# One sampling pass of four wide lag segments and one lag table, in place of two passes and two tables

## The chip, the cores and the metric

The kernel runs on one core of a Trainium2 chip. The metric is the device time in microseconds (us) of one execution. Engines are named as in the profile: PE (matrix products), DVE (elementwise work with two inputs, statistics), ACT (one-input functions, copies out of PSUM), POOL (GpSimd), SP (here only DMA issues). "PEclk" is the share of PE's full clock that was granted.

## The reference, cut to what matters

```python
# x: 1 x 2048 x 512, bf16; N = 128 states per channel
h  = x + A(layernorm(x))      # a state-space convolution over 2048 positions, per channel
h2 = h + B(layernorm(h))      # h @ w1 -> gelu -> @ w2, along the positions (2048 -> 1792 -> 2048)

# inside A, for each of 512 channels d:
P = exp(dt * A * l)                                # l = 0..2047
K = einsum("dn,dnl,dn->dl", C, P, dt * B).real     # the convolution kernel
y = causal_convolution(u, K) + u * Dskip           # by FFT in the reference
```

The kernel computes no FFT over 2048. It cuts the positions into 16 chunks of 128. Inside a chunk and its neighbour it works with exact spectra. Everything farther away goes through a **far field**: K is smooth enough in the lag to be interpolated from samples. The samples are taken on **segments** of the lag axis: around a segment's centre, K is a sum over the states of (a coefficient `cmu`) x (a table `T` of exponentials at 11 nodes). A product with a coefficient `mu` moves the centre one segment on.

Of the kernel before, what the change touches and what calls it, by code (L numbers as in the profile page):

```python
# [17 lines left out]
HR = 158.0  # L18
NR = 7
NQ = 11  # L20
NH = 5
QS = 12
NJ = 8
SEL0 = 100
SELW = 228
CA = 6
RA = 3
NA = (0, 6)
ROW = [QS * r if r < RA else 64 + QS * (r - RA) for r in range(NR)]
TQ = 88  # L30
# [18 lines left out]
def _tables():  # L49
    xh = np.cos(np.pi * np.arange(NH) / (NQ - 1))  # L50
    xh[2] = P / HR
    xq = np.concatenate([xh, -xh, [0.0]])
    tau = 63.5 + 64 * np.cos(np.pi * (2 * np.arange(NJ) + 1) / (2 * NJ))
    s = np.arange(P)
    om = np.pi * (2 * np.arange(64) + 1) / P
    co, si = np.cos(np.outer(s, om)), np.sin(np.outer(s, om))
    lb = _lagrange(tau, s)

    def wts(l):
        R = np.clip(np.floor(l / (2 * HR)), 0, NR - 1).astype(int)  # L60
        w = np.zeros((P,) + l.shape)
        for r in range(NR):
            w[ROW[r]:ROW[r] + NQ] = np.where(R == r, _lagrange(xq, (l - HR * (2 * r + 1)) / HR), 0)
        return w

    near = wts(s.astype(float))[:NQ]
    phi = [near @ co, near @ si]
    t = {}
    t["dft"] = np.concatenate([co, si], 1)
    t["lwin"] = np.zeros((P, 56))  # L70
    t["lwin"][:, 24:32] = lb.T
    selphi = np.zeros((P, 8, 2, P))
    selw = np.zeros((P, 8, SELW))
    for j in range(8):
        for q in range(NQ):
            for cs in range(2):
                selphi[8 * q + j, j, cs, 0:64] = phi[cs][q]
                selphi[8 * q + j, j, cs, 64:128] = phi[cs][q]
            selw[8 * q + j, j, SEL0 + q] = 1.0
    t["selphi"] = selphi.reshape(P, -1)  # L80
    t["selw"] = selw.reshape(P, -1)
    r = 15 - np.arange(16)
    wi = np.zeros((P, NJ, P))
    for i in range(NJ):
        lag = (128.0 * r[:, None] + tau[i] - tau[None, :]).reshape(-1)
        later = np.repeat(r > 0, NJ) * 1.0
        wi[:, i] = wts(lag + 128) + wts(np.maximum(lag, 0)) * later
    t["wi"] = wi.reshape(P, -1)
    t["inv1"] = np.concatenate([co.T, si.T], 0) / 64
    t["inv2"] = np.concatenate([si.T, -co.T], 0) / 64  # L90
    lrep = np.zeros((P, 4, P))
    for f in range(4):
        lrep[32 * f:32 * f + 32, f] = np.tile(lb, (4, 1))
    t["lrep"] = lrep.reshape(P, -1)
    off, cols = {}, []
    o = 0
    for k, v in t.items():
        off[k] = (o, v.shape[1])
        o += v.shape[1]
        cols.append(v)  # L100
    tab = np.concatenate(cols, 1).astype(ml_dtypes.bfloat16)
    msk = np.zeros((P, 4), np.float32)
    for p in range(P):
        msk[p, (p // 8) % 4] = 1.0
    return tab, off, msk, xh
# [54 lines left out]
class Op:  # L160
    __slots__ = ("i", "eng", "emit", "cost", "deps", "dma", "rd", "wr", "tag", "pos", "sig", "waits",
                 "mode", "name", "prio", "sec", "cols", "cw", "ins")


ENGINES = ("pe", "act", "dve", "pool", "sp")
LAT = 190.0
SAME = {"pe": 0.0, "act": 95.0, "dve": 125.0, "pool": 100.0, "sp": 0.0}
TICK = 10240 / 3
DMA_LAT = 1900.0
ISSUE = 480.0  # L170
MODE_NS = 70.0
TABLE_NS = 1280.0
RUN = 1024
RATE = {"raw": 275, "X": 275, "Mb": 275, "W2": 350}
WARM = (8000.0, 48000.0)


class Rec:



    def __init__(self, nc):
        self.nc = nc
        self.ops = []
        self.pages = {}
        self.bankops = {}
# [7 lines left out]
    def add(self, eng, emit, reads, writes, cost, dma=False, after=(), tag="", mode=None, name="", cols=0, share=1.0):  # L194
        o = Op()
        o.i = len(self.ops)
        o.eng, o.emit, o.cost, o.dma, o.tag, o.mode, o.name = eng, emit, cost, dma, tag, mode, name
        o.sec, o.cols, o.cw = self.sec + ":" + eng, cols, cols * share
        o.prio = PRIO.get(o.sec, self.base)
        if not name and writes and hasattr(writes[0], "tensor"):  # L200
            o.name = writes[0].tensor.name
        on_chip = lambda a: hasattr(a, "tensor") and not isinstance(a.tensor, bass.DRamTensorHandle)
        o.rd = [footprint(a) for a in reads if on_chip(a)]
        o.wr = [footprint(a) for a in writes if on_chip(a)]
        deps = set(x.i for x in after if x is not None)
        for is_w, fs in ((0, o.rd), (1, o.wr)):
            for f in fs:
                for b in banks(f):
                    for (q, qw) in self.bankops.get(b, ()):
                        if q in deps:  # L210
                            continue
                        if self.ops[q].eng != eng or eng == "pe" or is_w or qw:
                            deps.add(q)
                if f[0]:
                    continue
                for pg in self.pageset(f):
                    for (q, qw, qf) in self.pages.get(pg, ()):
                        if (is_w or qw) and q not in deps and overlap(f, qf):
                            deps.add(q)
        for is_w, fs in ((0, o.rd), (1, o.wr)):  # L220
            for f in fs:
                for b in banks(f):
                    self.bankops.setdefault(b, []).append((o.i, is_w))
                if not f[0]:
                    for pg in self.pageset(f):
                        self.pages.setdefault(pg, []).append((o.i, is_w, f))
        deps.discard(o.i)
        o.deps = sorted(deps)
        self.ops.append(o)
        return o  # L230
# [44 lines left out]
    def schedule(self):  # L275
        ops = self.nodes()
        n = len(ops)
        succ = [[] for _ in range(n)]
        for o in ops:
            for d in o.deps:  # L280
                succ[d].append(o.i)
        order = {e: [] for e in ENGINES}
        fin = [0.0] * n
        start = [0.0] * n
        nd = [len(o.deps) for o in ops]
        ready_t = [0.0] * n
        avail = {e: 700.0 for e in ENGINES}
        mode = {e: "exp" if e == "act" else None for e in ENGINES}
        dma_free = 0.0
        ticks = {}  # L290
        pend = {e: [] for e in ENGINES}
        for o in ops:
            if nd[o.i] == 0:
                pend[o.eng].append(o.i)
        left = n
        while left:
            best = None
            for e in ENGINES:
                if not pend[e]:
                    continue  # L300
                t0 = min(max(avail[e], ready_t[i]) for i in pend[e])
                if best is None or t0 < best[0]:
                    best = (t0, e)
            t0, e = best
            cand = [i for i in pend[e] if max(avail[e], ready_t[i]) <= t0]
            i = min(cand, key=lambda i: (ops[i].prio + (0 if ops[i].mode in (None, mode[e]) else 2), i))
            soon = [j for j in pend[e] if ops[j].prio < ops[i].prio - 0.3
                    and ready_t[j] < t0 + 0.5 * ops[i].cost and j not in cand]
            if soon and e != "pe" and not ops[i].dma:
                i = min(soon, key=lambda j: (ready_t[j], j))  # L310
            o = ops[i]
            pend[e].remove(i)
            t0 = max(t0, ready_t[i])
            if o.mode is not None and o.mode != mode[e]:
                t0 += MODE_NS if e == "pe" else TABLE_NS
                mode[e] = o.mode
            start[i] = t0
            cost = o.cost
            if e == "pe":
                tk = int(t0 // TICK)  # L320
                cost = o.cost if WARM[0] <= t0 < WARM[1] or ticks.get(tk - 1, 0) >= 3060 else o.cols
                ticks[tk] = ticks.get(tk, 0) + o.cw
            if o.dma:
                avail[e] = t0 + ISSUE
                dma_free = max(dma_free, t0) + o.cost
                fin[i] = dma_free + DMA_LAT
            else:
                avail[e] = t0 + cost
                fin[i] = t0 + cost
            order[e].append(i)  # L330
            left -= 1
            for s in succ[i]:
                nd[s] -= 1
                lat = SAME[e] if ops[s].eng == e and not o.dma else LAT
                ready_t[s] = max(ready_t[s], fin[i] + lat)
                if nd[s] == 0:
                    pend[ops[s].eng].append(s)
# [1035 lines left out]
```

## The kernel before: what the change and the argument touch

The segments are 316 lags wide (twice HR = 158), so 7 of them (NR) cover the axis. Coefficients `cmu` for segment r come from those of earlier segments by complex products with powers of mu, four of them single and one triple:

```python
# params(), on DVE; cuts marked ...
tt(m[:, :, :], SCm, bc2(Em), M)                 # mu^128
ts(self.p1[:, :], m[:, 0], 1.0, A)              # 1 + its real part
tt(self.num[:, :, :], self.cb[:, :, :], bc2(self.p1[:, :]), M)
tt(self.nb[:, :, :], self.cb[:, :, :], bc2(m[:, 1]), M)
tt(self.num[:, 0], self.num[:, 0], self.nb[:, 1], A)
tt(self.num[:, 1], self.num[:, 1], self.nb[:, 0], S)
...
for lv in range(3):                             # mu^2, mu^4, mu^8 by squaring
    ...
cprod(cm[:, :, 0:1], self.num[:, :, :].unsqueeze(2), 0, 1)
...
cprod(cm[:, :, 1:2], cm[:, :, 0:1], 1, 1)
cprod(cm[:, :, 2:3], cm[:, :, 1:2], 1, 1)
cprod(cm[:, :, 3:4], cm[:, :, 1:2], 2, 1)
cprod(cm[:, :, 4:7], cm[:, :, 0:3], 3, 3)
```

PE turns tables and coefficients into samples `g`, picks out the right ones with 0/1 matrices ("selections", `kt`), and interpolates a lag table `G` from them. G times the shifted moments `Mb` of the input gives the far field `O`. All this is done twice: segments 0 to 2 for the first 6 chunks, segments 3 to 6 for the other 10.

```python
def samples(self, hf):                          # hf = 0: three segments, hf = 1: four
    for nb in range(4):
        for gl in range(16):
            for c in range(2):
                mm(..., self.T[:, c, nb // 2, o:o + P], cm[:, c, 16 * nb + gl], ...)  # 128 products
        b.act(self.g[...], ...)                 # ACT copies them out of PSUM
    ...                                         # selections, copied into kt
def far(self, hf):
    for i in range(0, NJ, 2):                   # four pairs of nodes
        for q in range(2):
            b.mm(self.bank(bb + q), self.tb("wi", (i + q) * P, P), self.kt[:, :])
        b.act(dst, src, AF.Copy)                # G, 1024 columns, all four on ACT
    for s in range(32):
        for q in range(4):                      # the lag product, 128 small matmuls
            b.mm(..., Gv[:, q, s], Mv[:, q, s])
    ...                                         # O = result times a mask: 8 and 12 evictions, 12 of them on DVE
```

Behind it each chunk's output y takes the near product, the spectrum product and the far-field product on PE; DVE adds it to X; a second norm yields `H`; and H times the weights W1 and W2 fills PE to the end. The kernel orders its own instructions by a table of priorities.

## Time and profile before

The median of the three runs before the prediction was 164.92 us (164.78 to 165.16). The profiled execution is another one, with a span of 162.1 us.

| engine | busy us | what fills it |
|---|---|---|
| PE | 152.3 (94%) | real products, and 22.1 us of filler that reads only `idf`, all before 50 us |
| DVE | 139.7 | tables and coefficients in front, then y, norms and combinations of W1 |
| ACT | 84.6 | sines and exponentials, then PSUM evictions |
| POOL | 0.7 | nothing but constants |

There are 4062 instructions. I take the filler for no bound, since it stands where PE would otherwise wait.

### The profile page before, as it was taken

What the parts mean: (1) busy time and instruction counts of PE and PEld (TensorE: products, weight loads), DVE (VectorE), ACT (ScalarE), POOL (GpSimd) and SP (SyncE); (2) the same over time, 40 slices, a digit from 0 to 9 for tenths busy, and PEclk for the clock granted to TensorE, in tenths of its full rate; (3) what the DMA queues carried; (4) which work ended last, traced back from release to release, by engine and by line L of the source; (5) the groups of instructions that cost most, each with busy time, mean ns of one, the idle gap of its engine ahead of it and who ended that gap; (6) DMA issues with size and microseconds to landing.
All of it is one profiled execution on the core that took longest, in us unless ns stands there. A gap on an engine that the chain in (4) does not pass through costs nothing.

```text
span 162.1 us, 4062 instructions
## 1 busy us (share of the span) xinstructions
PE 152.3 (94%) x1705; PEld 112.9 (70%) x1705; DVE 139.7 (86%) x334; ACT 84.6 (52%) x201; POOL 0.7 (0%) x6
## 2 busy tenths in 40 slices
PE   7689958799989999999999999999999999999994
PEld 4569843468376753855544678888888888888883
DVE  3698999999999799999999999999999975384853
ACT  1799999898979899417467443158330000000000
POOL 1000000000000000000000000000000000000000
PEclk9999999999987999999999999999999999999999
DMA  4999999921407200069999000000000112102023
GB/s 122 349 383 401 400 405 398 405 91 53 145 20 239 93 0 0 4 210 418 406 411 363 14 0 0 0 4 0 0 0 4 34 42 89 34 32 69 32 69 126
DMA packets 12160, 23.78 MB, mean 147 GB/s; under 512 B 989, under 2 KB 8158, under 8 KB 12014
## 3 DMA queue, kind: packets, MB, share of 16 engines
q1 hardware_dynamic: 10558, 22.02, 36.6%
q10 hardware_dynamic: 1584, 1.51, 2.9%
q8 instruction: 13, 0.21, 0.5%
q14 instruction: 5, 0.04, 0.1%
HBM read 21.29 MB, written 2.35 MB: 146 GB/s over the span
## 4 chain that ended last, share of the span: by engine, by line
PE 68%; ACT 18%; DVE 10%; ACTq 1%; issue 1%
PE ps L485 68%; ACT SC L492 3%; DVE T L508 3%; ACT G L492 3%; DVE cmu L508 3%; ACT E L492 2%; ACT L498 2%; ACT H L492 2%; ACTq L542 1%; ACT junk L492 1%; DVE ct L508 1%; ACT g L492 1%; DVE X L522 1%; ACT kt L492 1%; ACT UF L492 1%
## 5 line engine op out<-in xcount | busy, mean ns | idle before, releaser
L485 PE MATMUL ps<-H,W 128*128 128x512 bf16 (+1 forms) x184 | 33.2, 328 | 0.0
L485 PEld LDWEIGHTS ps<-H,W 128*128 128x128 bf16 x184 | 17.4, 98 | 11.5 <-DVE H L518 0.9
L768 PE MATMUL ps<-idf 128*128 128x256 bf16 x154 | 22.1, 298 | 1.1 <-POOL idf L533 1.1
L485 PE MATMUL ps<-gT,W 128*128 128x256 bf16 x182 | 23.0, 273 | 0.0
L768 PEld LDWEIGHTS ps<-idf 128*128 128x128 bf16 x154 | 16.0, 107 | 4.9 <-POOL idf L533 1.1
L485 PEld LDWEIGHTS ps<-gT,W 128*128 128x128 bf16 x182 | 17.6, 98 | 2.2
L508 DVE TENSOR_TENSOR X<-ps,acc 128x256 bf16<-128x256 f32 x24 | 9.8, 421 | 7.2 <-PE ps L485 7.1
L508 DVE TENSOR_TENSOR W<-W 128x1024 bf16<-128x1024 bf16 (+1 forms) x23 | 14.7, 656 | 0.5 <-PE ps L485 0.4
L485 PE MATMUL ps<-HT,W 128*128 128x256 bf16 x112 | 14.2, 273 | 0.0
L522 DVE SCALAR_TENSOR_TENSOR acc<-ps,b2T,X 128x256 f32<-128x256 f32 x24 | 11.3, 478 | 3.1 <-PE ps L485 2.9
L492 ACT ACTIVATE H<-X 128x512 bf16<-128x512 bf16 x16 | 9.9, 619 | 5.5 <-DVE X L522 5.5
L522 DVE SCALAR_TENSOR_TENSOR X<-ps,X 128x512 bf16<-128x512 f32 x16 | 10.7, 687 | 1.4 <-PE ps L485 1.2
L485 PEld LDWEIGHTS ps<-HT,W 128*128 128x128 bf16 x112 | 10.9, 98 | 1.3
L485 PE MATMUL ps<-TS,S 128*128 128x256 bf16 x84 | 11.3, 273 | 0.0
L485 PE MATMUL ps<-TS,W 128*128 128x256 bf16 x84 | 11.0, 273 | 0.0
L492 ACT ACTIVATE UF<-ps,ub 128x512 bf16<-128x512 f32 x16 | 10.2, 685 | 0.6 <-PE ps L485 0.5
L492 ACT ACTIVATE snap<-ps 128x256 f32<-128x256 f32 x12 | 4.2, 384 | 10.1 <-PE ps L485 10.0
L485 PEld LDWEIGHTS ps<-TS,W 128*128 128x128 bf16 x84 | 8.1, 98 | 1.1 <-DVE acc L522 0.2
L485 PEld LDWEIGHTS ps<-TS,S 128*128 128x128 bf16 x84 | 8.1, 98 | 1.2
L485 PEld LDWEIGHTS ps<-cmu,T 128*128 128x128 bf16 x256 | 7.3, 98 | 2.0 <-ACT g L492 1.2
L492 ACT ACTIVATE gT<-ps,b1T 128x512 bf16<-128x512 f32 (+1 forms) x10 | 6.0, 602 | 4.2 <-PE ps L485 4.2
L485 PE MATMUL ps<-cmu,T 128*128 128x24 bf16 (+1 forms) x256 | 8.0, 178 | 0.2 <-ACT g L492 0.2
(125 smaller groups left out, 257.7 us busy)
## 6 DMA issues: line engine op xcount, KB each, us to landing
W<-in_B_w_dram SPq DMA_DIRECT2D x4, 1792.0 KB, 20.0
W<-in_B_w_dram SPq DMA_DIRECT2D x2, 2048.0 KB, 14.5
W<-in_B_w_dram SPq DMA_DIRECT2D x2, 1536.0 KB, 7.2
out_dram<-X SPq DMA_DIRECT2D x15, 128.0 KB, 1.7
tab<-tables SPq DMA_DIRECT2D x1, 1462.0 KB, 12.1
Mb<-ms_scratch SPq DMA_DIRECT2D x1, 1280.0 KB, 7.9
X<-in_A_u_dram SPq DMA_DIRECT2D x2, 512.0 KB, 5.7
X<-in_A_u_dram SPq DMA_DIRECT2D x1, 1024.0 KB, 9.1
```

The lines of the kernel that those rows point to most:

```text
L485: return self.r.add("pe", lambda e: e.matmul(out, lhsT=lhsT, rhs=rhs, start=start, stop=stop, skip_group_check=onto), [lhsT, rhs], [out], ...
L492: return self.r.add("act", lambda e: e.activation(out=out, in_=in_, func=func, bias=bias, scale=scale, accum_out=accum_out), [in_, bias, s ...
L498: return self.r.add("act", lambda e: e.preload_act_table_set(name), [], [], 10, mode=mode, tag="order", **k)
L508: return self.r.add(eng, lambda e: e.tensor_tensor(out=out, in0=a, in1=b, op=op), [a, b], [out], self._d(eng, nel(out), m), **k)
L522: return self.r.add(eng, lambda e: e.scalar_tensor_tensor(out=out, in0=a, scalar=s, in1=b, op0=op0, op1=op1, accum_out=accum_out), [a, s, ...
L542: return self.r.add(eng, lambda e: e.dma_start(out=out, in_=in_), [in_], [out], max(by / RATE.get(out.tensor.name.split("_")[0], 410) + 0. ...
L768: self.rec.hot = (hot, lambda e, bk: e.matmul(self.bank(bk, 0, 256), lhsT=hv[:, 0:P], rhs=hv[:, :], start=True, stop=True))
```

## The change

The intent: make the segments wide enough that four cover the whole lag axis, so that one sampling pass and one lag table serve all 16 chunks. That removes PE, ACT and DVE work between the first and the second half. Smaller parts go with it. The shift of the centre by 1 + mu^128 becomes one more exponential and sine and a sum. The four B*C products move to POOL. Two of the four G evictions move to DVE. The G products pack two 64-row halves into PE's rows. E and SC now lie where W1's last two quarters belong, so these are loaded later.

```diff
-HR = 158.0
-NR = 7
+HR = 273.0
+NR = 4
...
-tt(self.num[:, :, :], self.cb[:, :, :], bc2(self.p1[:, :]), M)
-tt(self.nb[:, :, :], self.cb[:, :, :], bc2(m[:, 1]), M)
-tt(self.num[:, 0], self.num[:, 0], self.nb[:, 1], A)
-tt(self.num[:, 1], self.num[:, 1], self.nb[:, 0], S)
+tt(self.t1[:, :, :], self.SC[:, :, NQ1], bc2(EX[:, 1]), M)
+tt(self.q[:, :, :], self.t1[:, :, :], mub[:, 0], A)
-for lv in range(3):
+for lv in range(2):
...
-cprod(cm[:, :, 2:3], cm[:, :, 1:2], 1, 1)
-cprod(cm[:, :, 3:4], cm[:, :, 1:2], 2, 1)
-cprod(cm[:, :, 4:7], cm[:, :, 0:3], 3, 3)
+cprod(cm[:, :, 2:4], cm[:, :, 0:2], mub[:, 2], 2)
...
-tt(bc[:, 0], rf(2), rf(3), M)
+tt(bc[:, 0], rf(2), rf(3), M, eng="pool", after=[diag])     # and the other three
...
-    b.mm(self.bank(bb + q), self.tb("wi", (i + q) * P, P), self.kt[:, :])
-b.act(dst, src, AF.Copy)
+    rows = slice(64 * q, 64 * q + 64)
+    b.mm(self.bank(bb + q), self.tb("wi", (i + q) * P, P)[rows], self.kt[rows], pack=2)
+if i in (2, 6):
+    b.ts(dst, src, 1.0, ALU.mult)
+else:
+    b.act(dst, src, AF.Copy)
...
-self.samples(1)
-self.far(1)          # table and lag product of the second half
+self.lag(1)          # only the lag product; the table is the first one
```

Cut here: the layout, the finer loads of X, the new priorities, the evictions of O (16, four of them on DVE, in place of 20 with twelve on DVE), and the norm statistics of the second half's chunks (four of eight on ACT, in place of six).

## The prediction

> **What bounds the kernel now.** I read the page's rows of busy tenths first, then the busy time of each engine in short stretches, then the chain of work that ended last, then the timelines of DVE, ACT and PE up to 95 us. The program has two parts. In the front the state-space parameters become sampled kernels and a far-field table; behind it come the convolution outputs (y), the second norm and the two matrix products.
>
> ```profile
> PE   7689958799989999999999999999999999999994
> DVE  3698999999999799999999999999999975384853
> ACT  1799999898979899417467443158330000000000
> ```
> A slice is 4.05 us. PE looks full nearly from the start, but that is partly deceptive: the 154 products that only read `idf` are filler, 22.1 us, all before 50 us. DVE and ACT are the full engines of slices 3 to 15.
>
> ```profile
> 10.00:15.00 5.00, 4.35 (x54) 3.83 (x53) 4.66 (x9) 4.98 (x9) 0.00 (x0) 1.00 1.05 404
> 30.00:35.00 5.00, 4.67 (x64) 3.19 (x65) 4.97 (x10) 4.49 (x10) 0.00 (x0) 1.00 0.70 270
> 45.00:50.00 5.00, 4.70 (x163) 3.78 (x163) 4.97 (x7) 3.70 (x9) 0.00 (x0) 0.76 0.12 29
> 130.00:140.00 10.00, 10.00 (x94) 8.87 (x92) 6.05 (x14) 0.00 (x0) 0.00 (x0) 1.00 0.16 54
> ```
> The columns after the stretch's length are PE, weight loads, DVE, ACT and POOL, then PE's granted clock and the DMA share. In the front POOL does nothing and DVE runs at 99%; at the end only PE is full.
>
> ```profile
> 7.68 5.48 ACT SC L492 x10
> 34.00 2.20 DVE T L508 x3
> 36.31 3.29 PE ps L485 x114
> 45.30 2.86 PE ps L485 x118
> 62.21 21.87 PE ps L485 x212
> 84.11 75.63 PE ps L485 x653
> ```
> This is the chain in order of time. ACT's sines start it, DVE's tables T and coefficients cmu carry it, then come samples, lag table G and the first lag product (45.30). From 62.21 to 159.73 it never leaves PE. So the end is the moment at which PE's backlog becomes continuous, plus that backlog. Two things can move it: an earlier start, or less PE work behind the start.
>
> ```profile
> 36.31 1.76 PE L485 MATMUL ps<-cmu,T 128*128 128x24 bf16 x64
> 45.30 2.72 PE L485 MATMUL ps<-Mb,G 128*32 128x24 bf16 x128 [0.63 <-ACT G L492]
> 48.36 1.15 PE L485 MATMUL ps<-cmu,T 128*128 128x32 bf16 x31
> 61.15 1.04 PE L485 MATMUL ps<-H,W 128*128 128x512 bf16 x4
> ```
> The first sampling pass (three segments) ends at 38.0 and the first lag product at 48.0; the second pass (four segments) runs from 48 to 55.4, mixed with the first y chunks; the first product with W1 starts at 61.15.
>
> **What the Trainium skill says.** "TensorE: Matmul & The Clock Gate", section "Wait — 56ns, not 53.3ns?", gives N / 2.4 GHz + about 2.5 ns between starts and a floor of about 25 ns for small N. The trace agrees: 62 sampling products of 24 columns took 1.72 us, so about 26 ns each, and 512 columns come every 0.215 us. Thus 32 columns instead of 24 cost PE almost nothing. "GPSIMD Engine Reference", "Engine selection", makes two-input elementwise work about twice as slow there as on DVE; "SBUF — State Buffer", "SBUF: two separate sides", says that the DVE and GpSimd share a port pair as an exclusive lock. No run shows this yet: POOL is busy for 0.7 us before. "ScalarE: Activation LUTs", "What ACT_TABLE_LOAD costs", gives 1283 ns a load, which is the 1283 ns mean of the three here; the extra drain it names doesn't show (the load at 13.17 follows a sine and is followed by an exponential at 14.46).
>
> **The change part by part.** Durations overlap on DVE and ACT, so I take start-to-start steps: two-input bf16 of 512, 1024, 1280, 2048 columns 0.34, 0.60, 0.735, 1.14 us; scalar_tensor_tensor of 512 0.60; one statistics pass 0.615; an ACT eviction of 512 about 0.5.
>
> DVE. Coefficient products: before four single ones (2 x 0.60 + 2 x 0.34 = 1.9) and a triple one (2 x 1.67 + 2 x 0.87 = 5.1), 12.7; after two single and one double (2 x 1.14 + 2 x 0.60 = 3.5), 7.3: minus 5.4. One doubling of mu less: minus 1.55. The centre shift loses 2.35 (num, nb, their two fix-ups, p1, half of m) and gains 1.2 (two of 1024): minus 1.15. The four B*C products go to POOL: minus 1.6. Three of eight diagonals go to ACT and a small one vanishes: minus 0.6. The output masks shrink from twelve to four evictions: minus 1.95. New: two of the four G evictions, 1024 columns each out of PSUM, 2.3 as an estimate from 0.688 for 512; two more norm statistics, 1.2. Sum: minus 8.7 us.
>
> ACT. Six G evictions less, 5.6; one sampling pass, 1.6; one kt, 0.5; two norm rows, 2 x 2 x (0.52 + 0.19) = 2.85. Added: two exponentials, one sine, three diagonals, four masks, about 3.2. Sum: minus 7.3 us. Five DMA issues also leave ACT's queue at the start (2.5 us, of which one stays), so its first table load can begin near 1.3 instead of 3.30, and dt is then bounded by its load, near 2.8 instead of 4.6.
>
> PE. 128 sampling products (3.3), 48 selections (1.3), the second G table (1.7) and half of the first by row packing (0.9) go.
>
> Not all of this is on the path. **The start:** DVE's work before the last T of 36.2 was 28.5 us. After, the single sampling pass needs all four coefficient segments first: plus 1.6 for the double product, plus 1.55 for a doubling that used to come later. Against that minus 1.15, 1.6 and 0.6 from above, and the second half's statistics (2 x 0.615) may come later. So the path's DVE work stays near 28 us, and only its beginning moves, by 1 to 2 us. I put the last T at 34.5 (36.1 before). From there before took 11.8 us to the end of the first lag product. After: 64 samples 1.7, eviction 0.9 with its hand-offs, 32 selections 0.9, kt 0.9, G in two rounds on two engines 2.4 instead of four on one (5.2 with kf and the interposed small ones), lag 2.8, remaining hand-offs 0.4: 10.0. The first lag product ends near 44.5 instead of 48.0: 3.5 us earlier.
>
> **The backlog behind it,** before, by counts and steps: the second half's spectra 8 x 0.215 = 1.7; second samples 3.3; selections 0.9; second G 1.7; second lag 3.2; y 16 x (3 x 0.215) = 10.3; first product 96 x 0.215 = 20.6; the Strassen-like blocks (224 + 392) x 0.1067 = 65.7. Sum 107.4; 159.7 - 48.0 = 111.7, so 4.3 us were gaps or reduced clock (0.76 and 0.90 in 45 to 55). After: 107.4 - 5.9 (samples, selections, G) - 0.2 = 101.3. Gaps: before, the stretch from 48.0 to 61.15 held 11.5 us of work in 13.2; after there is less to fill the same latency from the first y eviction to the first product with W1 (54.44 to 61.15, 6.7 us). I therefore raise 4.3 to 5.5. So PE ends at 44.5 + 101.3 + 5.5 = 151.3. The span adds 2.4 behind PE (162.1 - 159.7) and the measured median 2.8 on the span: 156.5 us, minus 8.4 (5%).
>
> **The rivals.** (1) *No earlier start.* T and the sines are untouched, four segments must be ready at once, and 11 sines now follow three exponentials, so the last table load comes some 1.3 us later. Then only the PE work counts: 164.9 - 5.9 + 1.2 = 160.2. For it: the near-equal DVE sum above. Against it: the shorter G stage is off DVE's sum. (2) *A transfer takes the place.* W1's last two quarters lie on E and SC now and can only be loaded when T is done, 3.67 MB, about 9 us at the 400 GB/s seen in 10 to 30 us; the Mb copies of the shifted moments may share the engines with them. If the first copy queues behind, the lag product waits up to 8 us and the time is 163 to 165. Against it: moments are ready near 30 us before, ahead of T. (3) *DVE becomes the bound of the y stretch.* Before, it needed 54.4 to 86.7 for it and PE finished that stretch near 94.4, so 8 us of slack; six of them go with the removed PE work, but masks (1.95) leave it and products no longer delay it. If it binds, 158 to 159. (4) *POOL late or in DVE's way.* An estimate from the GPSIMD page's 2.6 cycles an element is 1.1 us a product of 512; done near 10 us, cb is needed only at some 15 us. Worth at most 2 us. (5) *A better gain:* if second-half spectra and lag fit into PE's idle front, up to 3.5 us more: 153.
>
> **Range and chances.** Two thirds of the gain (5.9 us of PE work) is arithmetic that only a new gap can undo; the start is what I know worst, 2.5 us either way. Rivals 1 and 3 lie at 158 to 160, rival 5 at 153, rival 2 outside. So 152.8 to 160.6; faster by over 2% (below 161.6) 0.92, within 2% 0.07, slower 0.01.
>
> **What would show it.** In the changed trace: one block of 128 products of 32 columns on cmu and T; POOL with five products before 12 us; the last T at 33 to 36; G's evictions on ACT and DVE side by side, and the first lag product's end at 43 to 46.5; the first product with W1 at 52 to 55; PE then full to the end. Wrong would make it: a lag product waiting for Mb, PE idle for over 3 us between first lag product and first W1 product, or the last norm outputs H arriving after PE asks for them, near 83.

## The result, and the profile after

The changed kernel took 156.11 us (median of 4 runs, 155.38 to 157.02), the kernel before 164.85 us in the same rounds (4 runs, 164.19 to 165.16). The ratio is 0.9478, with a 95% interval of 0.9414 to 0.9541. Ratios here are the mean time of one kernel's fast runs over that of the other's fast runs of the same rounds, so not quite the ratio of the medians.

The page of the changed kernel, busy times and then busy tenths in slices of 3.87 us:

```profile
span 154.7 us, 3685 instructions
PE 143.5 (93%) x1522; PEld 106.7 (69%) x1529; DVE 131.4 (85%) x308; ACT 78.2 (51%) x192; POOL 6.7 (4%) x11
...
PE   7849869989998889999999999999999999999993
...
DVE  5099999998999998999999999957999994558663
ACT  4897999998997868614544832545320000000000
```

DVE lost 8.3 us of busy time (139.7 to 131.4) and ACT 6.4 (84.6 to 78.2). In the second DVE slice stands a 0 that was a 6 before: DVE now waits for X there. PE is below 9 in slices 13 to 15 (46 to 58 us), where it was at 9 before.

The stretches of the changed kernel that stand against two shown of before, with the same columns:

```profile
30.00:35.00 5.00, 4.51 (x78) 3.65 (x77) 5.00 (x7) 4.97 (x16) 0.00 (x0) 1.00 0.67 210
45.00:50.00 5.00, 4.33 (x132) 3.26 (x126) 4.72 (x9) 3.89 (x9) 0.00 (x0) 1.00 0.40 134
```

From 30 to 35 us DVE is as full as it was. PE's clock in 45 to 50 us is 1.00 instead of 0.76, though PE has less to do there.

The chain of waits of the changed kernel: start, length, what.

```profile
9.19 12.65 DMA tab<-tables
...
25.82 3.68 DVE T L522 x5
...
33.76 3.49 PE ps L499 x126
...
40.21 1.94 ACT G L506 x2
...
44.93 3.14 DMA ms_scratch<-ms
...
48.09 6.31 DMA Mb<-ms_scratch
...
54.44 2.85 PE ps L499 x114
57.29 0.16 issue
57.45 7.54 PE ps L499 x49
...
81.83 70.49 PE ps L499 x621
```

From 57.45 PE is never released by anything but itself: 94.9 us to 152.3. Before, that began at 62.21. The load that the chain names first, 12.65 us, looks like a bound. An experiment below finds no gain in taking it earlier. Ahead of the second lag product (54.44) the chain goes through the copies of the shifted moments, but PE waited only 0.27 us for them. In the control below, the same instructions in another execution, the chain goes through DVE's y work there instead. So two paths of nearly equal length meet at that product.

PE between the last table and the first product with W1:

```profile
33.76 3.49 PE L499 MATMUL ps<-cmu,T 128*128 128x32 bf16 x126
37.95 1.57 PE L499 MATMUL ps<-g,tab 128*128 128x64 bf16 x48
39.78 0.82 PE L499 MATMUL ps<-kt,tab 64*128 64x512 bf16 x6
42.22 0.39 PE L499 MATMUL ps<-kt,tab 64*128 64x512 bf16 x2
44.57 2.86 PE L499 MATMUL ps<-Mb,G 128*32 128x32 bf16 x128
49.65 0.62 PE L499 MATMUL ps<-O,tab 128*128 128x128 bf16 x8 [0.52 <-DVE O L530]
54.44 2.85 PE L499 MATMUL ps<-Mb,G 128*32 128x32 bf16 x128 [0.27 <-DMA Mb<-ms_scratch]
57.45 0.81 PE L499 MATMUL ps<-H,W 128*128 128x512 bf16 x3 [0.16 <-issue]
```

One block of samples is left instead of two, and no second block on kt follows the y chunks. The fourth pair of G products (42.22) comes 2.4 us behind the first six. The first lag product ends at 47.43, only 0.6 us earlier than before (48.0). The first product with W1 comes 3.7 us earlier (61.15 to 57.45), and PE's end 7.4 us earlier (159.73 to 152.32).

Which engine fills the stretch ahead of that product? The 8 us from 50 to 58, first before, then after:

```profile
50.00:58.00 8.00, 7.83 (x161) 5.72 (x161) 7.06 (x16) 7.48 (x18) 0.00 (x0) 0.94 0.49 160
```

```profile
50.00:58.00 8.00, 7.01 (x161) 5.02 (x160) 8.00 (x21) 6.11 (x20) 0.00 (x0) 1.00 0.33 112
```

Before, PE was the fullest (7.83), with ACT close behind (7.48). After, DVE is busy for all of the 8.00 us and PE has room. **The fullest engine of this stretch was PE and is now DVE.** Whether the removed PE work did that is for an experiment to say.

### The profile page after: what moved, and what is told of

It reads as the page before. It is cut to its first block, busy times and chain, and to the rows that moved or that the text cites. A ratio compares the mean times of both kernels' runs of the same rounds, so it can differ in the third digit from the quotient of the medians.

```text
span 154.7 us, 3685 instructions
## 1 busy us (share of the span) xinstructions
PE 143.5 (93%) x1522; PEld 106.7 (69%) x1529; DVE 131.4 (85%) x308; ACT 78.2 (51%) x192; POOL 6.7 (4%) x11
## 4 chain that ended last, share of the span: by engine, by line
PE 67%; DMA 14%; DVE 7%; SPq 5%; ACT 3%; issue 2%
PE ps L499 67%; DMA tab<-tables 8%; SPq L556 5%; DMA Mb<-ms_scratch 4%; DVE T L522 3%; DVE cmu L522 3%; DMA ms_scratch<-ms 2%; ACT G L506 1%; DVE ct L522 1%; ACT UF L506 1%; PE ps L784 1%; ACT ms L506 0%; ACT kf L506 0%; DVE X L536 0%; ACT mb L506 0%
## 5 line engine op out<-in xcount | busy, mean ns | idle before, releaser
L499 PE MATMUL ps<-H,W 128*128 128x512 bf16 (+1 forms) x180 | 32.5, 327 | 0.3 <-issue 0.2
L499 PEld LDWEIGHTS ps<-gT,W 128*128 128x128 bf16 x182 | 17.0, 98 | 3.0 <-DVE X L522 0.2
L506 ACT ACTIVATE gT<-snap,b1T 128x256 bf16<-128x256 f32 x12 | 6.0, 505 | 9.1 <-DVE snap L522 9.1
L542 DVE BATCH_NORM_STATS2 st<-X 128x6 f32<-128x512 bf16 x12 | 7.4, 679 | 3.5 <-DMA X<-in_A_u_dram 3.5
L506 ACT ACTIVATE gT<-ps,b1T 128x512 bf16<-128x512 f32 (+1 forms) x10 | 5.4, 606 | 4.7 <-PE ps L499 4.7
L499 PEld LDWEIGHTS ps<-O,tab 128*128 128x128 bf16 x64 | 4.8, 98 | 3.9 <-DVE O L530 0.8
```

The costliest lines, as they stand in the source:

```text
L499: return self.r.add("pe", lambda e: e.matmul(out, lhsT=lhsT, rhs=rhs, start=start, stop=stop, skip_group_check=onto), [lhsT, rhs], [out], ...
L506: return self.r.add("act", lambda e: e.activation(out=out, in_=in_, func=func, bias=bias, scale=scale, accum_out=accum_out), [in_, bias, s ...
L542: return self.r.add("dve", lambda e: e.bn_stats(out=out, in_=a), [a], [out], 67 + nel(a) / 0.96, **k)
```

## The experiments

**How they were built.** The kernel schedules itself, so any edit could reshuffle hundreds of instructions. Each experiment therefore replays the order of the changed kernel on every engine, and only adds or moves the named instructions. Without edits, this gave the same instructions in the same order with the same waits. They ran on three chips, so I compare by each kernel's ratio to the kernel before on its own chip. The first time given for each kernel is the median of all its runs, slow ones included; the ratios use fast runs alone. "Against the control" means the difference of two such ratios times 164.9 us. With 95% half-widths of about 0.0057 for the control and 0.004 to 0.009 for the others, such a difference is good to about 1.2 us (up to 1.8 us where the other is widest). A profile is one execution: where its front began early or late by chance, I say so. All outputs were correct.

**The theories.** Mine: the gain is the removed PE work, and PE has no room to hide it. The rivals: DVE's front sets the time; loads set it; or the new order leaves a hole that a better order would close.

### Control: the same instructions, replayed

```diff
-r.schedule()
+r.replay(order_of_the_changed_kernel)
```

> The changed kernel, its instruction order frozen so that later edits move nothing else. Both theories: the same order and waits as the changed kernel, 155.4 to 157.0 us, first lag product ending near 47.4 us, first product with W1 near 57.5 us.

156.59 us (156.12 to 157.67, 4 runs) against 164.14 before; ratio 0.9556 (0.9499 to 0.9612). The last T, the first lag product and the first product with W1 lie within 0.4 us of the changed kernel's. The ratio is 0.008 above that of the first measurement, and the two intervals overlap. The control is the base for what follows.

### Put the removed PE work back

```diff
+for n, columns in ((128, 32), (32, 64), (8, 512)):   # 5.9 us: samples, selections, G
+    for i in range(n): b.mm(spare_bank, tb("dft"), cmu[..., columns])   # between O and acc0
 self.lag(1)
```

> The changed kernel with PE work of the size of the removed second pass (128 products of 32 columns, 32 of 64, 8 of 512; 5.9 us by the steps of before) put back between the first lag product and the first product with W1, into a bank nobody reads. Theory A (the gain is the PE backlog that went away, partly turned into idle PE while y, norm and H are awaited): PE is idle for about 3.6 us there now, so the end moves by 5.9 less what fits into idle, plus 2.5 to 6 us, 158.5 to 162. Rival B (the gain is the relief of DVE and ACT, PE's removed work was in gaps): less than 1 us, 156 to 157.

162.36 us (median; three fast runs 162.12 to 162.52, one slow at 165.09); ratio 0.9880 (0.9832 to 0.9928). That is 5.3 us against the control, for 5.9 us of dummy products that nobody waits for; the control's own gain on this chip was 7.3 us. In the profile, the first lag product and the first product with W1:

```profile
46.05 2.87 PE L582 MATMUL ps<-Mb,G 128*32 128x32 bf16 x128
63.49 0.81 PE L582 MATMUL ps<-H,W 128*128 128x512 bf16 x3 [0.16 <-issue]
```

In the control they start at 44.57 and 57.13. So of the 6.4 us by which the second comes later, 1.5 stand ahead of the first added product (48.86) and are not the edit's: in this execution PE's granted clock was 0.50 from 23 to 26 us, where the control had 1.00. That leaves 4.9 us by the profile. By the times, the run of this kernel at a clock of 1.000 (162.19) is 6.1 us above the control's (156.12). The price lies near the 5.9 us in each reading. The 50 to 58 us stretch of this kernel:

```profile
50.00:58.00 8.00, 7.37 (x159) 5.59 (x161) 5.57 (x14) 5.81 (x15) 0.00 (x0) 1.00 0.40 135
```

DVE's busy time fell from 8.00 to 5.57 though DVE's own work did not change. Part of that is the late front: 1.5 us later, from 51.5 to 59.5, it is 6.56. In PE's order the added products stand ahead of y products, so y reaches DVE later. With the work back, PE is the fuller engine again (7.37 in both stretches), as before the change. This carries my main step: **PE work in this stretch costs nearly its full length**, and it did so although the changed kernel had 2.7 us of idle PE there by the count below (the expectation said 3.6). One limit: I chose the places of the added products. A scheduler might have put some of them into the gaps.

### Put DVE work ahead of the tables

```diff
+for i in range(3):                     # 1.85 us, behind the second coefficient product
+    b.bn(self.xst[:, 0:6], self.X[:, i])
```

> The changed kernel with three more statistics passes (3 x 0.615 = 1.85 us) on DVE ahead of the tables T. If DVE's order of work up to the last T sets the start, and the start sets the end, the last T, the first lag product and the end all move by 1.8 us: 157.5 to 158.5. If the first part has slack (the tables wait for ACT or for a load) or the idle PE behind the first lag product absorbs it: less than 1 us.

159.02 us (158.24 to 159.35); ratio 0.9675 (0.9626 to 0.9723): 2.0 us against the control. The first product with W1 came at 60.27, 3.1 us later than the control's 57.13:

```profile
60.27 0.81 PE L582 MATMUL ps<-H,W 128*128 128x512 bf16 x3 [0.16 <-DVE H L615]
```

Of the 3.1 us, 2.25 stand at the first lag product already (46.82 against 44.57) and 0.78 are a wait for the second copy of the shifted moments, the other path named above. So DVE's front is on the path too, at about its own length. This and the run before do not contradict each other: the path runs through DVE until the last T, and through PE and DVE in turn behind it.

### The load that the chain names

```diff
 # order of SP's loads
+load(tab, the 46 KB part that Fs reads)
 load(b1, b2, Dskip), load(zeros), load(W1[0:4]), load(X[8:12]), load(tab, 1296 KB part)
-load(tab, the 46 KB part that Fs reads)
```

> The changed kernel with one transfer moved: the 46 KB table with the transform and window (it landed at 21.8 us, 12.7 us after its issue, behind W1's first quarter and the large tables) issued ahead of the biases. Theory: DVE's norm scaling no longer waits there, but DVE waited only 0.2 us and the centre rows of cmu still wait for ACT, so 0 to 0.7 us faster. Rival (the load is what the start hangs on, as the chain of work says with 12.65 us on it): 1 us faster or more.

156.32 us (156.19 to 156.47); ratio 0.9517 (0.9479 to 0.9556): 0.6 us below the control, inside the uncertainty. So the 12.65 us at the head of the chain were not to be had. The chain names what was released last; in the changed kernel DVE had waited for this load for 0.19 us only. It has no slack, though: in other executions DVE waited longer for the same load, 0.51 us in the control, 0.99 in the run with the PE work back and 1.06 in the last one below. Whether tenths of a microsecond can be had there stays open.

### X ahead of C in the loads

```diff
 # order of SP's loads
-A_re, B_im, B_re, C_re, X[0:4], C_im, X[4:8], (small ones), W1[0:4], X[8:12], tab
+A_re, X[0:4], B_im, B_re, C_re, X[4:8], C_im, tab (46 KB), (small ones), W1[0:4], ...
```

> The changed kernel with the loads in another order: the first X pieces ahead of the B and C parameters, the small table ahead of the biases. DVE sat idle for 3.5 us until 7.55 waiting for X. If the start of DVE's work sets the last T, it comes 1 to 2 us earlier (33.2 to 34.2 instead of 35.2) and so does the end: 154.0 to 155.5. If ACT (11 sines, then the exponentials after the table load at 17.4) sets it, T moves by less than 0.5 us and the end stays.

158.80 us (fast runs 156.92 and 158.17, two slow ones); ratio 0.9684 (0.9600 to 0.9767): no gain, by its ratio rather 2.1 us slower. DVE started at 5.05 instead of 7.55, as intended. Then POOL waited instead:

```profile
7.23 2.26 POOL L609 TENSOR_TENSOR bc<-raw 128x512 bf16<-128x512 bf16 x2 [5.87 <-DMA raw<-in_A_C_re_dram]
```

In the changed kernel that row starts at 5.56. Here the coefficients cb came at 15.84 (14.81 in the control), the third table load of ACT at 18.48 (17.08), and the last T ended at 35.70 (35.17 in the changed kernel). What X gained here, C lost. This does not show that DVE's late start is harmless. In the next two runs on the same chip, which leave the loads and the front alone, X happened to land earlier than in the control: DVE's statistics started at 6.04 and 6.07 (7.23 in the control), and the last T ended at 33.99 and 34.36 (35.17). That points to X being on the path; no run brings X earlier without delaying C.

### The G stage rearranged

```diff
 # order on PE
-G4, G2, G0, u9, u8, (second-half norm products), G6, (moments), u11, u10, lag
+G0, G4, G2, u9, u8, G6, (second-half norm products), (moments), lag, u10, u11
 # on DVE: G6 ahead of the spectra product; on ACT: G0 ahead of G4, u10 and u11 behind
```

> The changed kernel with the four evictions of the lag table G drawn together: the pair that fills the reused bank first on PE and ACT, the last pair ahead of the second half's norm products, the last eviction ahead of the spectra's products on DVE, two spectra behind the lag product. The prediction took 2.4 us for this stage, the trace shows 4.3. Theory: the first lag product ends 0.6 to 1.5 us earlier (46.0 to 46.8), the end follows by half of it or less, since PE is idle behind it anyway: 155 to 156.2. Rival (start and end move one to one): 154.5 to 155.5.

157.68 us (fast runs 156.80 to 158.24, one slow); ratio 0.9563 (0.9496 to 0.9630): no difference from the control. The first lag product ended at 46.39, 1.1 us earlier. But the last T had ended 1.2 us earlier too (33.99), ahead of the edit, with X. The stage itself did not get shorter: from the kt copy's end (38.5) to the last G eviction (43.3) it took 4.8 us, where the changed kernel took 4.3. DVE now waited for the fourth pair of G products, which stood behind two spectra on PE:

```profile
42.07 1.22 DVE L622 TENSOR_SCALAR G<-ps 128x1024 bf16<-128x1024 f32 x1 [1.31 <-PE ps L591]
```

And ACT evicted the two spectra u10 and u11 between the lag product and y, so that y's first products with O came at 50.35 (49.68 in the control) and the first product with W1 at 57.59 (57.13). So the run tells nothing of what a shorter stage is worth: that was not built.

### H ahead of the filling work on DVE

```diff
 # order on DVE
-... V sums, y0..y3, a spectrum product, H0..H3
+... y0..y3, H0..H3, V sums, the spectrum product
```

> The changed kernel with DVE's sums of W1 (three of 0.6 us) and the products of the spectra for the third group (2 x 1.14 us) moved behind the first four normalised chunks H, and one spectrum eviction moved behind the first y squares on ACT. Theory: behind the first lag product PE waits for H, which DVE makes late because other work stands in front; H comes 2 to 3 us earlier, the idle PE of about 3.6 us shrinks, and the end moves by 1 to 2.5 us: 153.5 to 155. Rival (PE there waits for the second copy of the shifted moments, which lands at 54.4, since the second lag product stands before the first product with W1): less than 0.5 us.

161.31 us (fast runs 159.04 to 161.42, one slow); ratio 0.9756 (0.9666 to 0.9845): 3.3 us slower than the control. My build was poor: two y evictions, and the small steps of the next norm, now stood behind 4 us and more of moved work on DVE. The profile fell in a slow run, so I take no small difference from it. But a large one stands in it: the first product with W1 came at 56.35, 0.8 us ahead of the control's, and then PE stood still for about as long as the whole loss:

```profile
63.04 2.31 PE L587 MATMUL ps<-H,W 128*128 128x512 bf16 x5 [3.25 <-ACT O L594]
```

That mask stands on ACT behind a norm step for which ACT waited 3.44 us, until DVE's small step at 62.01.

### The last three edits together

> The three edits of loads, ylat and gstage together. If they are additive: 2.5 to 5 us faster than the changed kernel, 151 to 153.5. If the copy of the second half's shifted moments becomes the wait (it was bound at 54.4 already), at most 2 us: 154 to 155.5.

The edit is the sum of the three above. 166.16 us (165.86 to 166.92); ratio 1.0103 (1.0049 to 1.0158): slower than the kernel before, and 9.0 us behind the control, more than the three single losses (2.1 + 0.1 + 3.3). ACT waited for the coefficients:

```profile
16.80 1.02 ACT L609 ACTIVATE cb<-ps 128x1024 bf16<-128x1024 f32 x1 [2.49 <-PE ps L602]
```

and, where POOL's last two products ran beside two-input work of DVE, both took longer than elsewhere (first DVE, then POOL):

```profile
12.06 1.61 DVE L625 TENSOR_TENSOR mub<-SC,E 128x1024 bf16<-128x1024 bf16 x1
13.59 1.12 DVE L625 TENSOR_TENSOR sm<-sm 128x8 f32<-128x8 f32 x1
```

```profile
7.63 2.26 POOL L625 TENSOR_TENSOR bc<-raw 128x512 bf16<-128x512 bf16 x2 [6.27 <-DMA raw<-in_A_C_re_dram]
...
11.45 3.23 POOL L625 TENSOR_TENSOR bc<-raw 128x512 bf16<-128x512 bf16 x2
```

The same DVE product takes 0.69 us in the changed kernel, and the 8-column one 0.17. The last T ended at 38.54. Three edits, none of which helped alone, did not become helpful together.

### A second lag table

```diff
+for i, engine in ((0, act), (2, dve), (4, act), (6, dve)):   # G again, behind y3 and y5
+    ...same products and evictions as far()...
 self.lag(1)
```

> The changed kernel with the lag table G computed and evicted a second time, from the same samples, between the fourth y chunk and the second lag product (one part of the change undone): 8 row-packed products (0.9 us of PE), two evictions on ACT (1.9) and two on DVE (2.3). If a second table stands in the way (the second lag product waits for its last eviction and the first product with W1 stands behind it): 2 to 4.5 us slower than the changed kernel, 158.5 to 161. If it hides beside the y chunks: less than 1 us.

161.68 us (161.16 to 162.74); ratio 0.9819 (0.9776 to 0.9862): 4.3 us against the control, though the products themselves are eight, packed by two (0.91 + 0.61 us on PE in its trace). The rest is a wait:

```profile
59.37 2.84 PE L582 MATMUL ps<-Mb,G 128*32 128x32 bf16 x128 [2.93 <-DVE G L613]
```

PE stood for 2.93 us at the second lag product until DVE, the full engine of this stretch, had done the last eviction. Of the parts taken singly, sharing one table is the largest that I measured. In this build most of what it saves is the hand-off and not the products. The size holds for this order and this split of evictions; before, all four evictions were on ACT.

### The centre shift worked out on its own

```diff
+act(nat(self.sx2), W[1], AF.Sin, scale=128.0)        # one more sine
+tt(self.m1, EX[:, 0], self.sx2, M); ts(self.p1, self.m0, 1.0, A)
-tt(self.t1, self.SC[:, :, NQ1], bc2(EX[:, 1]), M); tt(self.q, self.t1, mub[:, 0], A)
+tt(num, self.cb, bc2(self.p1), M); tt(nb, self.cb, bc2(self.m1), M); two fix-ups
```

> The changed kernel with the centre shift undone: 1 + mu^128 applied to the coefficients on its own as before (one more sine on ACT, 0.6 us; on DVE 2.4 us of instructions in place of 1.2). If DVE's work ahead of the tables sets the end, as three extra statistics passes showed (2.4 us for 1.85): 1.2 to 2 us slower, 157.5 to 158.6. If DVE has slack there: less than 0.7 us.

157.88 us (fast runs 157.07 to 158.23, one slow, which is the profiled one); ratio 0.9564 (0.9520 to 0.9608): 0.1 us against the control, good to 1.2 us. Its worth is between nothing and about 1 us, and these runs cannot tell where.

### The B*C products back on DVE

```diff
-tt(bc[:, 0], rf(2), rf(3), M, eng="pool")
+tt(bc[:, 0], rf(2), rf(3), M, eng="dve")             # and the other three
```

> The changed kernel with the four products of B and C back on DVE, between its first norm statistics (1.6 us), POOL idle. If DVE's sum sets the start: 1.6 to 2.2 us slower, 158 to 158.8. If DVE only loses time that it spends waiting (3.2 us for X, a load at 21.8)[...]: less than 0.7 us.

157.71 us (156.96 to 157.97); ratio 0.9563 (0.9525 to 0.9600): again 0.1 us, good to 1.2. The last T ended at 36.03, 0.9 us later than in the control. Moving 1.6 us of DVE work to POOL bought at most about 1 us, and my runs do not resolve it from nothing. The 1.85 us of the statistics above cost more, 2.0; both figures are good to 1.2 us only, and the two stand in different places of DVE's order.

### The y stretch rearranged

```diff
 # masks of the first half: bank 0 on ACT, bank 1 on DVE; on DVE: y before the V sums
 # and spectra products; on PE: the second lag product behind the first products with W1
-O(0..3) by column group, V, y, spectra, H ... lag(1), W1
+O by bank, y, H, V, spectra ... W1 (three), lag(1)
```

> A version that may beat the changed kernel, after the badly built ylat (it put two y evictions behind 4 us of other DVE work): the masks of the first lag product split by bank, one on ACT and one on DVE; DVE's sums of W1 and third group of spectra products behind the first H; the second lag product behind the first six products with W1. Theory: y starts 0.5 to 1 us earlier, the first product with W1 comes near 54.5 instead of 57.3, PE's 3.6 us of idle time there shrink by 1 to 2.5 us: 154 to 155.5. Rival (ACT's squares and the norm's small steps set the time to H): first W1 product not before 56, less than 0.7 us.

162.56 us (8 runs; fast ones 160.64 to 163.03); ratio 0.9831 (0.9792 to 0.9871): 4.5 us slower than the control. DVE in this kernel:

```profile
51.65 0.69 DVE L632 SCALAR_TENSOR_TENSOR X<-ps,X 128x512 bf16<-128x512 f32 x1 [1.44 <-PE ps L595]
...
55.61 0.16 DVE L618 TENSOR_TENSOR sm<-s,sm 128x4 f32<-128x4 f32 x1 [0.98 <-ACT H L602]
56.91 0.73 DVE L628 TENSOR_SCALAR H<-X,sm 128x512 bf16<-128x512 bf16 x2 [1.14 <-ACT sm L602]
```

The first lag product started 1.6 us late in this profile (46.20 against 44.57), before any edited instruction: the granted clock was 0.50 from 24 to 27 us, so I don't put all 4.5 us down to the edit. Counted from the end of the lag product, H comes hardly sooner than in the changed kernel: 7.9 us (49.04 to 56.91) against 8.1 (47.43 to 55.55). DVE stands idle in the hand-offs between y, the square on ACT, the small steps and H. In the changed kernel the V sums and spectra products fill these waits; moved behind H, they had to be done later. From 57 to 82 us PE was busy for 21.6 of 25.0 us (24.7 in the control), and its longest wait there, 1.63 us at 74.66, was for an H that DVE made behind the V sums.

## Why the prediction was right, point by point

The time was right, and so was its main cause, the removed PE work. But the split was not: 3.5 of the 8.4 us were to come from an earlier start and 4.9 from a smaller backlog. Between the two profiled executions PE's end moved by 7.4 us, 0.6 from the start and 6.8 from the backlog. Against the prediction the start was 2.9 us late, the backlog 1.9 us short and the last term 1.0 us short. That these cancel to 0.03 us is luck. The ledger, all from the profiled execution, which took 156.53 us:

| step | predicted | measured |
|---|---|---|
| last T done | 34.5 | 35.17 |
| from there to the end of the first lag product | 10.0 | 12.26 |
| first lag product ends | 44.5 | 47.43 |
| backlog behind it, to PE's last product | 106.8 | 104.89 |
| PE's last product ends | 151.3 | 152.32 |
| behind it to the span's end | 2.4 | 2.4 |
| span to time | 2.8 | 1.8 |
| time | 156.5 | 156.53 |

**"The start ... 3.5 us earlier" was wrong: it came 0.6 us earlier.** Two terms failed. For 0.7 of the 2.9 us, the front's beginning did not move by 1 to 2 us as I put it: DVE's statistics started at 7.55, 0.6 us later than before (6.95), and waited 3.5 us for X. The run with X first does not settle whether this can be undone. For the other 2.3 us, the G stage, put at 2.4 us, took 4.3 us, from the kt copy's end (39.7) to the last G eviction (44.0). On DVE a product of spectra ran between its two evictions:

```profile
40.44 1.22 DVE L530 TENSOR_SCALAR G<-ps 128x1024 bf16<-128x1024 f32 x1
...
41.65 1.22 DVE L522 TENSOR_TENSOR Pb<-UF,kf 128x2048 bf16<-128x2048 bf16 x1
42.78 1.22 DVE L530 TENSOR_SCALAR G<-ps 128x1024 bf16<-128x1024 f32 x1
```

and the fourth pair of G products stood behind other products in PE's order. I had counted durations and not the other work in the order of the engines. My one try at that stage did not shorten it, so what repairing it is worth stays open.

**The removed PE work was right.** 5.9 us were predicted from counts and steps, and putting as much back cost 5.3 us against the control. **Rival 1,** no earlier start, was nearly right about the start. Its third table load even came 4.2 us later (13.17 to 17.40, not 1.3), while the first T stayed where it was (25.77 before, 25.74 after). That the time lies well below its 160.2 is due to the backlog, which shrank by 6.8 us and not by 4.7.

**The backlog was 1.9 us shorter than predicted.** Before it was 111.7 us (159.73 - 48.0), after 104.9. Four of the eight second-half spectra (4 x 0.215 = 0.86 us) now stand ahead of the first lag product in PE's order; my sum had all eight behind it. (Two stood ahead of it in the kernel before already, at 39.93, so my 107.4 us of work there were 0.4 too many and its gaps 4.7 us.) That leaves 101.3 - 0.86 = 100.4 us of work by my counts and 4.5 us of gaps, where I had raised the gaps to 5.5. Of the gaps 2.7 us lie before the first product with W1: 10.02 us from 47.43 to 57.45 hold 4 spectra, 11 other products of 512 columns (15 x 0.215), 24 of 128 columns (1.3) and the lag product (2.8), 7.3 us in all. So the gap behind the first y was there, as I had expected, but I had made it too large.

**The span-to-time term was off by 1.0 us.** I had subtracted the span of one execution from the median of others. That execution was itself fast, 163.83 us, so the right difference was 1.7. This error and the one in PE's end cancelled. The same applies to the gain: by the profiled executions it is 7.3 us (163.83 to 156.53), by the ratio 8.6.

**Rival 2,** a wait for the shifted moments: it did not come. The second copy arrived at 54.40 and PE waited 0.27 us; in no profile did PE wait over 0.8 us for it. PE shows no wait for the late quarters of W1. **Rival 3,** DVE as the bound of the y stretch: half right. DVE is full from 50 to 58, and 23.0 of 24.0 us from 58 to 82 (22.9 before). But PE is full there too (23.84), so it cost no visible wait once the products with W1 had begun. The slack shrank: the last H is done at 82.60, and the products with the last chunks of H start about 84. Before it was 86.7 against about 92. The next PE saving in this stretch will meet DVE. **Rival 4,** POOL late: its products ended at 11.65, later than my 10, and cb was evicted at 15.13; moving them back cost at most about 1 us. While POOL worked, DVE ran one-input statistics (7.55 to 12.40), so the case of the run with three edits did not arise. **Rival 5,** second-half spectra in PE's idle front, came true for the four spectra above, two more than before: 0.4 of its 3.5 us.

**The signs.** One block of samples, POOL's five products before 12 us, the last T, G's evictions on two engines and a PE that stays full came as named. Two did not: the first lag product ended at 47.43 (named: 43 to 46.5), and the first product with W1 came at 57.45 (52 to 55). Between them PE was idle for 2.7 us, just under the 3 us that I had called a sign of being wrong.

**The sums and readings.** DVE lost 8.3 us (predicted 8.7) and ACT 6.4 (7.3). I misread two lines: DVE's 99% in front holds for two of the stretches shown, 30 to 35 and 45 to 50; from 10 to 15 it is 93% (4.66 of 5.00). And 1.72 us over 62 products is 27.7 ns each, with the length of the last one in it; from start to start, 64 of them took 1.62 us (36.31 to 37.93), 25.3 ns each. The conclusion held: 126 products of 32 columns took 3.49 us, 27.7 ns each by the first way of counting.

**What stays open.** PE's clock in the profiled executions was 0.989 before and 1.000 after, with 0.62 between 48 and 52 us before. In the same rounds as the control, runs of the kernel before at 0.968 or 0.969 took 164.15 to 164.96 us and those at 0.979 or 0.989 took 163.69 to 164.14. On the other two chips the order is not so clean: 165.10 and 165.20 at 0.990 beside 164.69 at 0.969 on one, 165.23 and 165.41 at 0.979 beside 164.51 at 0.969 on the other. So some tenths of the gain, perhaps up to 1 us, may come with the clock; no run separates that. The two late fronts above show that a stretch at 0.50 can cost 1.5 us when it falls ahead of the first lag product. No run took DVE work out of the 50 to 58 us stretch, so that DVE bounds it rests on its busy share and on the added PE work. The worth of the row packing and of W1's late load was not measured. I found no version faster than the changed kernel by more than the uncertainty.

## What to carry to other kernels

Find the moment from which one engine never waits again, and price a change as "how much earlier does that moment come" plus "how much less stands behind it"; then check each half by adding the removed work back. Where two engines hand work to and fro, durations are not enough: walk through each engine's order and see what stands between the two hand-offs, because that is what the next step waits for. A transfer named at the head of the chain of waits is a candidate and no verdict, and work that fills an engine's waits should stay where it is unless the wait itself goes. Check that an edit did what it was built for before reading its time: here a stage that should have got shorter got longer, and an earlier front hid it.

## What the Trainium skill lacked or had wrong

- "GPSIMD Engine Reference", section "Engine selection": it puts two-input elementwise work at about twice the time of DVE. Here a bf16 product of 512 columns took POOL 1.13 us and DVE 0.34 us a step, 3.3 times as long. It calls one-input work roughly line-rate; the one-input multiplication by a constant took 1.49 us for the same 512 columns, longer than the two-input product:

```profile
5.56 2.27 POOL L522 TENSOR_TENSOR bc<-raw 128x512 bf16<-128x512 bf16 x2 [4.20 <-DMA raw<-in_A_C_re_dram]
7.92 1.49 POOL L530 TENSOR_SCALAR raw<-raw 128x512 bf16<-128x512 bf16 x1
```

- "SBUF — State Buffer", section "SBUF: two separate sides": the exclusive lock between DVE and GpSimd is stated in words, the loser blocked for the other's whole instruction, without a length for a pair of two-input products. In the run with three edits, the two engines' overlap made a pair of POOL products 0.97 us longer (3.23 against 2.26), one DVE product 0.92 us longer (1.61 against 0.69) and an 8-column one 0.95 us longer (1.12 against 0.17). That agrees with the lock; the trace shows the lengths and not the lock itself.
- "ScalarE: Activation LUTs", section "What ACT_TABLE_LOAD costs": the 1283 ns of a load agree, but the further drain of about 1380 ns did not show. In the changed kernel the third load began at 17.40, as the sine before it ended (17.39), and the first exponential behind it at 18.70, 1.30 us later.
- None of the pages that I read says how to weigh the chain of waits: it put 12.65 us on a load, and taking that load earlier moved the time by 0.6 us, which is within the uncertainty.
